# A convolution's weight-gradient loads moved ahead of the last input-gradient stage, with twelve row buffers in place of four

## The chip, the cores and the metric

One core of a Trainium2 chip. The metric is the device time of one execution in microseconds (us); each figure is the median of several executions. The kernel before takes 2702.24 us (5 runs, 2699.1 to 2705.55).

## The reference

A strided 1-D convolution, a normalisation over time, GELU, and the gradients of all of it. B = 2 batches, T = 16000 samples, 256 channels, K = 31 taps, stride 2, L = 7985 outputs.

```python
for i in range(K):                               # forward
    h += einsum('blc,cd->bld', x[:, i:i+s*L:s, :], w[i])
h = (h - mu) / sqrt(var + 1e-5) * gn_gamma + gn_beta
return gelu(h)
# and its vector-Jacobian product with grad_out: gradients of x, w, gamma, beta
```

## The kernel before

It runs in three phases, all bound to TensorE. Forward convolution of batch 0, then of batch 1 (the elementwise work of batch 0 runs beside it); input-gradient convolution of batch 0 (the elementwise work of batch 1 beside it), then of batch 1; weight gradient in four segments. TensorE is called PE in the views, ScalarE ACT, VectorE DVE, GpSimd POOL and SyncE SP. The tiles named most: `pt`, the PSUM banks into which TensorE transposes; `row`, `xrow` and `wrow`, rows in SBUF on their way out (results and intermediates, input gradient, weight gradient); `osl` and `gT`, what is transposed for out_0 and gh_dram; `w_sb` and `wT_sb`, the weights of phase 1 and 2; `xg` and `gseg`, the two operands of one weight-gradient segment; `sg`, a sigmoid. The pools:

```python
# phase 1 and 2: pools, on two sides of SBUF; "stg" holds rows on their way out
big   = tc.tile_pool(name="big",   bufs=3)                     # left side
wpool = tc.tile_pool(name="wpool", bufs=1,  side="right")      # w_sb, later wT_sb
xtp   = tc.tile_pool(name="xtp",   bufs=16, side="right")
temps = tc.tile_pool(name="temps", bufs=2,  side="right")
otp   = tc.tile_pool(name="otp",   bufs=4,  side="right")
stg   = tc.tile_pool(name="stg",   bufs=4,  side="right")      # tags "row" and "xrow"
ps_tr = tc.tile_pool(name="ps_tr", bufs=2, space=PSUM)         # pt
...
def transpose_and_store(srcs, b, l0, N, dram_dst):             # out_0 and gh_dram
    for q in range(_cdiv(N, P)):
        pt = ps_tr.tile([P, NDD, P], BF16, name="pt")
        for dd in range(NDD):
            nc.tensor.transpose(out=pt[0:M, dd, :], in_=srcs[dd][...], identity=ident[:])  # L262
        row = stg.tile([P, D], BF16, name="row")
        nc.scalar.copy(out=row[0:M, :], in_=pt[...])                                       # L264
        nc.gpsimd.dma_start(out=dram_dst[...], in_=row[0:M, :])                            # L265
...
def conv_backward_x(b):                                        # input gradient, L480
    ...  # 30 or 32 matmuls into acc_x; scalar.copy to xrow (L489); gpsimd store (L490)
...
# the elementwise work of the last batch: a slab's transposes follow its arithmetic by "lag" steps
items_last = new_sched(elementwise_items(last), lag=8)
# phase 3, after those pools are closed
seg = tc.tile_pool(name="seg", bufs=2, side="right")
for b in range(B):
    for h in range(NH):
        xg   = seg.tile([P, RW, C], BF16, name="xg")           # 46.5 KB a partition
        gseg = seg.tile([P, SH, D], BF16, name="gseg")         # 16 KB a partition
        ...  # six loads of gseg from gh_dram (L574), six of xg from x (L582), on the SP queue
        for grp in groups:                                     # 8 taps, one PSUM bank each
            ...  # matmuls acc_w (L600); VectorE adds into gw_acc, the last segment into wrow
```

A scheduler orders each engine's instructions from this program and places the waits by the addresses that tiles share. A pool that is opened later over the addresses of a closed one waits for the last use of what lay there.

## Time and profile before

| what (kernel before) | us | where to read it |
|---|---|---|
| span | 2701.7 | page |
| PE busy | 2611.7 (97%) | page |
| PE waits for xg, once | 25.3 | waits of PE |
| PE waits for rows leaving pt, 26 times | 25.9 | waits of PE |
| ScalarE waits for row stores | 27.5 + 7.6 | waits of ACT |

A busy TensorE cannot be made shorter by this change, since no matmul is removed. What can be won is its idle time, and the slow clock after idle time. So the first view to read is the waits of PE in the kernel before: who waited for whom, us in total, times, longest.

```profile
PE pt L262 <- ACT row L264: 25.9, 26, 3.9
PE acc_w L600 <- DMA xg<-in_x_dram: 25.3, 1, 25.3
PE acc_f L212 <- DMA w_sb<-in_w_dram: 9.7, 1, 9.7
PE acc_w L600 <- DVE wrow L618: 6.5, 3, 2.5
PE acc_x L480 <- DMA wT_sb<-in_w_dram: 3.1, 3, 2.5
```

The same view for ScalarE (ACT) says what most of the first line is: the copy out of pt has no free row to write to until an earlier row has reached memory.

```profile
ACT row L264 <- DMA gh_dram<-row: 27.5, 33, 2.5
...
ACT row L264 <- DMA out_dram<-row: 7.6, 5, 2.1
```

The second line of PE is one event. The chain of waits of the kernel before (start, length, what) shows it step by step: the last output store lands, only then does the SP queue issue the loads, 22 us later the data is there.

```profile
1784.41 1.78 DMA out_dram<-xrow
1786.19 0.02 SPq L574
...
1786.88 21.98 DMA xg<-in_x_dram
...
1808.99 51.09 PE acc_w L600 x452
```

The windows view of the kernel before (window, its length, then busy time and count of PE, PEld, DVE, ACT, POOL, then the granted clock, DMA share, GB/s) shows that the stall goes on costing after it ended: the clock has dropped to 0.50, and the first matmuls run at half pace (10 in 2 us, later 21).

```profile
1805.00:1809.00 4.00, 0.01 (x1) 0.04 (x2) 0.00 (x0) 0.00 (x0) 0.00 (x0) 0.50 0.29 122
1809.00:1811.00 2.00, 2.00 (x10) 1.45 (x11) 0.00 (x0) 0.00 (x0) 0.00 (x0) 0.50 0.33 126
1811.00:1813.00 2.00, 2.00 (x15) 1.54 (x14) 0.00 (x0) 0.00 (x0) 0.00 (x0) 0.68 0.32 129
1813.00:1815.00 2.00, 2.00 (x21) 1.80 (x19) 0.00 (x0) 0.00 (x0) 0.00 (x0) 1.00 0.32 126
```

The same view with windows cut at five events gives the stages. The events are the first gh_dram transpose, the last transposes of out_0, the last transposes of gh_dram, the end of the input gradient, and the first weight-gradient matmul.

```profile
0.00:865.30 865.30, 846.16 (x4018) 394.16 (x4096) 263.65 (x763) 136.30 (x379) 36.50 (x79) 1.00 0.29 58
865.30:1234.40 369.10, 347.09 (x3172) 303.67 (x3171) 263.43 (x757) 114.41 (x293) 118.48 (x218) 0.98 0.20 50
1234.40:1317.50 83.10, 78.66 (x757) 68.70 (x757) 0.00 (x0) 28.11 (x85) 44.78 (x85) 1.00 0.22 67
1317.50:1784.00 466.50, 466.17 (x4264) 417.99 (x4263) 0.00 (x0) 51.82 (x140) 75.88 (x141) 1.00 0.07 21
1784.00:1809.00 25.00, 0.01 (x1) 0.04 (x2) 0.00 (x0) 0.12 (x1) 6.82 (x2) 0.59 0.28 111
1809.00:2701.70 892.70, 873.65 (x7936) 778.56 (x7936) 81.37 (x155) 0.00 (x0) 39.42 (x63) 0.99 0.11 38
```

In the second stage lies one more stall worth a look, from the order of instructions in time (start, length, engine, line, what, and in brackets the idle time before it and its releaser): PE waits 3.86 us for a row copy, and ScalarE, which owes it, had itself been idle for 5.91 us, waiting for VectorE.

```profile
972.42 0.63 ACT L286 ACTIVATE sg<-inner 128x512 bf16<-128x512 bf16 x1 [5.91 <-DVE inner L283]
...
973.20 0.65 ACT L264 COPY row<-pt 128x256 bf16<-128x256 bf16 x2
...
973.63 0.37 PE L262 MATMUL pt<-ident,osl 128*128 128x128 bf16 x2 [3.86 <-ACT row L264]
```

### The profile page before, as it was taken

How to read it: one execution, taken by the hardware profiler on the slowest of the kernel's cores; microseconds unless marked ns; L12 is line 12 of the kernel's file. 1: busy time of each engine (PE TensorE's matmuls, PEld its weight loads, DVE VectorE, ACT ScalarE, POOL GpSimd, SP SyncE). 2: the span in 40 equal slices, each digit the busy share in tenths (PEclk: the TensorE clock that was granted, in tenths of full speed). 3: DMA queues.
4: the chain of work that ended last, by engine and by line, in shares of the span. 5: the costliest groups of instructions: out<-in, count | busy, mean ns of one | idle time of the engine just before them, and what ended most of it. 6: DMA issues, size and time to landing. Idle time of an engine off the chain costs nothing.

```text
span 2701.7 us, 45421 instructions
## 1 busy us (share of the span) xinstructions
PE 2611.7 (97%) x20143; PEld 1963.1 (73%) x20220; DVE 608.4 (23%) x1675; ACT 330.8 (12%) x895; POOL 321.9 (12%) x586
## 2 busy tenths in 40 slices
PE   8999999999999899999999999969999999999997
PEld 3444445444445688888888888858888888888886
DVE  0000005755571886770000000000001000100001
ACT  0010102222211522222211111100000000000000
POOL 0000000000001522234411111110000000000112
PEclk9999999999999999999999999989999999999999
DMA  5212123432225401111100000022102002100000
GB/s 113 45 38 43 39 40 69 80 59 45 55 55 104 102 30 34 32 34 51 52 20 20 19 20 22 22 77 102 68 1 120 1 1 64 57 1 1 17 17 30
DMA packets 221422, 121.51 MB, mean 45 GB/s; under 512 B 198218, under 2 KB 206188, under 8 KB 220724
## 3 DMA queue, kind: packets, MB, share of 16 engines
q1 hardware_dynamic: 202984, 81.74, 12.8%
q0 software_dynamic: 18240, 36.85, 4.6%
q8 instruction: 158, 2.59, 0.4%
q14 instruction: 40, 0.33, 0.0%
HBM read 36.04 MB, written 36.82 MB: 27 GB/s over the span
## 4 chain that ended last, share of the span: by engine, by line
PE 69%; issue 20%; POOL 4%; DVE 2%; DMA 2%; ACT 1%; SPq 0%; POOLq 0%; ACTq 0%; DVEq 0%
PE acc_w L600 26%; PE acc_x L480 24%; PE acc_f L212 18%; POOL gh_dram L265 1%; POOL out_dram L620 1%; DMA gh_dram<-row 1%; POOL out_dram L490 1%; DMA xg<-in_x_dram 1%; POOL out_dram L265 1%; ACT row L264 1%; PE pt L262 0%; DMA out_dram<-row 0%; DVE gT L355 0%; DVE junk_v L362 0%; DVE inner L283 0%
## 5 line engine op out<-in xcount | busy, mean ns | idle before, releaser
L600 PE MATMUL acc_w<-gseg,xg 125*128 125x256 bf16 x7936 | 873.7, 273 | 32.0 <-DMA xg<-in_x_dram 25.3
L480 PE MATMUL acc_x<-wT_sb,gT 128*128 128x256 bf16 (+1 forms) x7812 | 882.0, 274 | 3.1 <-DMA wT_sb<-in_w_dram 3.1
L600 PEld LDWEIGHTS <-xg 125*128 125x128 bf16 x7936 | 778.6, 98 | 127.0 <-issue 33.3
L212 PE MATMUL acc_f<-xt,w_sb 128*128 128x512 bf16 (+1 forms) x3891 | 840.5, 374 | 13.8 <-DMA w_sb<-in_w_dram 9.7
L480 PEld LDWEIGHTS <-gT 128*128 128x128 bf16 (+1 forms) x7812 | 762.3, 98 | 90.7 <-issue 5.0
L212 PEld LDWEIGHTS <-w_sb 128*128 128x128 bf16 x3968 | 385.0, 97 | 453.4 <-DMA w_sb<-in_w_dram 9.7
L490 POOL DMA_DIRECT2D out_dram<-xrow x252 | 137.0, 544 | 634.7 <-ACT xrow L489 564.9
L612 DVE COPY gw_acc<-acc_w 128x512 f32<-128x512 f32 x31 | 18.9, 682 | 805.9 <-PE acc_w L600 805.9
L489 ACT CAST xrow<-acc_x 128x256 bf16<-128x256 f32 (+1 forms) x252 | 93.3, 371 | 614.9 <-PE acc_x L480 603.3
L265 POOL DMA_DIRECT2D out_dram<-row x126 | 68.0, 545 | 811.8 <-ACT row L264 801.4
L614 DVE TENSOR_TENSOR gw_acc<-acc_w,gw_acc 128x512 f32<-128x512 f32 x62 | 37.8, 683 | 396.3 <-PE acc_w L600 396.3
L237 DVE TENSOR_REDUCE hsum<-hsum_part 128x2 f32<-128x32 f32 x2 | 0.4, 186 | 477.6 <-ACT hT L221 477.6
L221 ACT ACTIVATE hT<-acc_f 128x512 bf16<-128x512 f32 (+1 forms) x64 | 37.5, 586 | 550.4 <-PE acc_f L212 550.4
L264 ACT COPY row<-pt 128x256 bf16<-128x256 bf16 (+1 forms) x252 | 86.6, 379 | 45.4 <-DMA gh_dram<-row 27.5
L620 POOL DMA_DIRECT2D out_dram<-wrow x62 | 33.1, 539 | 413.5 <-DVE wrow L618 412.6
L265 POOL DMA_DIRECT2D gh_dram<-row x126 | 67.7, 543 | 42.7 <-ACT row L264 35.0
L618 DVE TENSOR_TENSOR wrow<-acc_w,gw_acc 128x256 bf16<-128x256 f32 x62 | 24.6, 422 | 207.5 <-PE acc_w L600 186.1
L561 POOL MEMSET xg<- 32x7424 bf16 x2 | 12.6, 6279 | 453.8 <-PE acc_w L600 452.0
L288 DVE TENSOR_TENSOR osl<-z,sg 128x512 bf16<-128x512 bf16 (+1 forms) x64 | 25.1, 416 | 175.8 <-PE pt L262 164.8
L286 ACT ACTIVATE sg<-inner 128x512 bf16<-128x512 bf16 (+1 forms) x64 | 39.7, 621 | 166.8 <-DVE inner L283 158.2
L262 PE MATMUL pt<-ident,gT 128*128 128x128 bf16 (+1 forms) x252 | 32.5, 222 | 17.9 <-ACT row L264 16.6
L340 ACT ACTIVATE sg<-inner 128x512 bf16<-128x512 bf16 (+1 forms) x64 | 39.7, 621 | 74.5 <-DVE inner L337 72.5
(73 smaller groups left out, 761.7 us busy)
## 6 DMA issues: line engine op xcount, KB each, us to landing
out_dram<-xrow POOLq DMA_DIRECT2D x248, 64.0 KB, 1.8
out_dram<-row POOLq DMA_DIRECT2D x124, 64.0 KB, 2.6
gh_dram<-row POOLq DMA_DIRECT2D x124, 64.0 KB, 1.8
gseg<-gh_dram SPq DMA_DIRECT2D x16, 375.0 KB
xg<-in_x_dram SPq DMA_DIRECT2D x8, 750.0 KB
xg<-in_x_dram SPq DMA_DIRECT2D x8, 744.0 KB
xg<-in_x_dram SPq DMA_DIRECT2D x2, 2312.5 KB
xg<-in_x_dram SPq DMA_DIRECT2D x2, 2294.0 KB
```

The costliest lines, as they stand in the source:

```text
L212: nc.tensor.matmul(accs[dd][:, 0:N], lhsT=w_sb[:, cc, i, dd * P:(dd + 1) * P], rhs=rhs, start=(n == 0), stop=(n == total - 1),)
L221: nc.scalar.activation(out=hT_b[:, dd, PADL + l0:PADL + l0 + N], in_=accs[dd][:, 0:N], func=ACT.Copy, accum_out=hsum_part[b][:, dd, lt:lt ...
L264: nc.scalar.copy(out=row[0:M, :], in_=pt[0:M].rearrange("p k d -> p (k d)"))
L265: dma_out.dma_start(out=dram_dst[b, l0 + c0:l0 + c0 + M, :], in_=row[0:M, :])
L286: nc.scalar.activation(out=sg[:, 0:N], in_=inner[:, 0:N], func=ACT.Sigmoid, scale=GELU_K)
L340: nc.scalar.activation(out=sg[:, 0:N], in_=inner[:, 0:N], func=ACT.Sigmoid, scale=GELU_K)
L480: nc.tensor.matmul(acc[0:Mu, 0:C], lhsT=gT_b[:, dd, PADL + u0 - m:PADL + u0 - m + Mu], rhs=wT_sb[:, dd, i, :], start=(n == 0), stop=(n == ...
L489: nc.scalar.copy(out=xrow[0:Mu, :], in_=acc[0:Mu, 0:C])
L490: dma_out.dma_start(out=out_1[b, bass.ds(2 * u0 + par, Mu, step=2), :], in_=xrow[0:Mu, :])
L600: nc.tensor.matmul(accs[ti][:, cc, :], lhsT=xg[0:NG, 2 * s + i, cc * P:(cc + 1) * P], rhs=gseg[0:NG, s, :], start=(cnt[ti] == 0), stop=(cn ...
L614: nc.vector.tensor_tensor(out=dst, in0=src_ps, in1=dst, op=ALU.add)
L620: dma_out.dma_start(out=out_2[i, cc * P:(cc + 1) * P, :], in_=wrow[:])
```

## The change

Its intent: load the first weight-gradient segment while the last input gradient still runs, into the space of the elementwise pools, which are no longer needed by then; and give the rows on their way out more buffers. To make the room, the weights and the rows move to the left side, and the two segment buffers become two pools. The loading code moves into a function, unchanged, and stg3, the pool of wrow, moves to the left too (both cut).

```diff
-        wpool = ph12.enter_context(tc.tile_pool(name="wpool", bufs=1, side="right"))
-        xtp = ph12.enter_context(tc.tile_pool(name="xtp", bufs=16, side="right"))
-        temps = ...; otp = ...                                  # side="right"
-        stg = ph12.enter_context(tc.tile_pool(name="stg", bufs=4, side="right"))
+        wpool = ph12.enter_context(tc.tile_pool(name="wpool", bufs=1))
+        stg = ph12.enter_context(tc.tile_pool(name="stg", bufs=12))
+        phE = ExitStack()                    # xtp, temps, otp: closed early
+        xtp = phE.enter_context(tc.tile_pool(name="xtp", bufs=16, side="right"))
+        temps = ...; otp = ...
 ...
             else:                            # last batch
+                phE.close()
+                segA = tc.alloc_tile_pool(name="segA", bufs=1, side="right")
+                segA_holder[0] = segA
+                seg_first[0] = bw_load_segment(segA, *bw_segments[0])
                 for _ in conv_backward_x(b):
                     pass
 ...
-        seg = ph3.enter_context(tc.tile_pool(name="seg", bufs=2, side="right"))
+        segB = tc.alloc_tile_pool(name="segB", bufs=1, side="right")
+        seg_pools = [segA, segB]             # segments take turns; the first one is already loaded
```

More of the change, by code (lines that the diff above doesn't have):

```diff
@@ L119, with bw_load_segment @@
             r0 += rn
+    GRP = 8
+    groups = [list(range(i0, min(K, i0 + GRP))) for i0 in range(0, K, GRP)]
+    def bw_load_segment(pool, b, h):
+        xg = pool.tile([P, RW, C], BF16, name="xg", tag="xg")
+        gseg = pool.tile([P, SH, D], BF16, name="gseg", tag="gseg")
+        g_last = NG - 1
+        max_r_last = T - 1 - (2 * SB * g_last + 2 * SH * h)
+        nfull = NG if max_r_last >= RW - 1 else NG - 1
+        if nfull < NG:
+            qb0 = (g_last // 32) * 32
+            r_inv0 = max(0, max_r_last + 1)
+            nc.gpsimd.memset(xg[qb0:qb0 + 32, r_inv0:RW, :], 0.0)
+        s_bounds = sorted(set([0] + [min(SH, v) for v in (4, 8, 14, 20, 26)] + [SH]))
+        r_prev = 0
+        for pi in range(len(s_bounds) - 1):
+            s_lo, s_hi = s_bounds[pi], s_bounds[pi + 1]
+            if s_hi <= s_lo:
+                continue
+            r_hi = min(RW, 2 * (s_hi - 1) + K)
+            gsrc = bass.AP(
+                tensor=gh_dram.tensor,
+                offset=gh_dram[b, SH * h + s_lo, 0].offset,
+                ap=[[SB * D, NG], [1, (s_hi - s_lo) * D]],
+            )
+            dma_in.dma_start(out=gseg[0:NG, s_lo:s_hi, :].rearrange("g s d -> g (s d)"), in_=gsrc)
+            if r_hi > r_prev:
+                if nfull > 0:
+                    src = bass.AP(
+                        tensor=x.tensor,
+                        offset=x[b, 2 * SH * h + r_prev, 0].offset,
+                        ap=[[2 * SB * C, nfull], [1, (r_hi - r_prev) * C]],
+                    )
+                    dma_in.dma_start(out=xg[0:nfull, r_prev:r_hi, :].rearrange("g r c -> g (r c)"), in_=src)
+                if nfull < NG:
+                    nv = min(max_r_last + 1, r_hi)
+                    if nv > r_prev:
+                        t0 = 2 * SB * g_last + 2 * SH * h
+                        dma_in.dma_start(
+                            out=xg[g_last:g_last + 1, r_prev:nv, :],
+                            in_=x[b, t0 + r_prev:t0 + nv, :].rearrange("(o r) c -> o r c", o=1),
+                        )
+                r_prev = r_hi
+        return xg, gseg
@@ L121 @@
+    bw_segments = [(b, h) for b in range(B) for h in range(NH)]
+    seg_first = [None]
+    segA_holder = [None]
     with ExitStack() as ph12:
         big = ph12.enter_context(tc.tile_pool(name="big", bufs=3))
-        wpool = ph12.enter_context(tc.tile_pool(name="wpool", bufs=1, side="right"))
-        xtp = ph12.enter_context(tc.tile_pool(name="xtp", bufs=16, side="right"))
-        temps = ph12.enter_context(tc.tile_pool(name="temps", bufs=2, side="right"))
-        otp = ph12.enter_context(tc.tile_pool(name="otp", bufs=4, side="right"))
@@ L131 @@
+        temps = phE.enter_context(tc.tile_pool(name="temps", bufs=2, side="right"))
+        otp = phE.enter_context(tc.tile_pool(name="otp", bufs=4, side="right"))
         w_sb = wpool.tile([P, NCC, K, D], BF16, name="w_sb", tag="w")
@@ L530 @@
             else:
+                phE.close()
+                segA = tc.alloc_tile_pool(name="segA", bufs=1, side="right")
+                segA_holder[0] = segA
+                seg_first[0] = bw_load_segment(segA, *bw_segments[0])
                 for _ in conv_backward_x(b):
                     pass
+        phE.close()
     ggam_bf = const.tile([P, NDD], BF16, name="ggam_bf")
@@ L543 @@
         accp = ph3.enter_context(tc.tile_pool(name="accp", bufs=1))
-        seg = ph3.enter_context(tc.tile_pool(name="seg", bufs=2, side="right"))
-        stg3 = ph3.enter_context(tc.tile_pool(name="stg3", bufs=4, side="right"))
+        stg3 = ph3.enter_context(tc.tile_pool(name="stg3", bufs=4))
+        if segA_holder[0] is None:
+            segA_holder[0] = tc.alloc_tile_pool(name="segA", bufs=1, side="right")
+        segA = segA_holder[0]
+        segB = tc.alloc_tile_pool(name="segB", bufs=1, side="right")
@@ L546 @@
         ps_w = ph3.enter_context(tc.tile_pool(name="ps_w", bufs=8, space=bass.MemoryType.PSUM))
-        GRP = 8
-        groups = [list(range(i0, min(K, i0 + GRP))) for i0 in range(0, K, GRP)]
         gw_acc = accp.tile([P, K, NCC * D], FP32, name="gw_acc")
-        first_seg = True
-        for b in range(B):
-            for h in range(NH):
-                xg = seg.tile([P, RW, C], BF16, name="xg", tag="xg")
-                gseg = seg.tile([P, SH, D], BF16, name="gseg", tag="gseg")
-                g_last = NG - 1
-                max_r_last = T - 1 - (2 * SB * g_last + 2 * SH * h)
-                nfull = NG if max_r_last >= RW - 1 else NG - 1
-                if nfull < NG:
-                    qb0 = (g_last // 32) * 32
-                    r_inv0 = max(0, max_r_last + 1)
-                    nc.gpsimd.memset(xg[qb0:qb0 + 32, r_inv0:RW, :], 0.0)
-                s_bounds = sorted(set([0] + [min(SH, v) for v in (4, 8, 14, 20, 26)] + [SH]))
-                r_prev = 0
-                for pi in range(len(s_bounds) - 1):
-                    s_lo, s_hi = s_bounds[pi], s_bounds[pi + 1]
-                    if s_hi <= s_lo:
-                        continue
-                    r_hi = min(RW, 2 * (s_hi - 1) + K)
-                    gsrc = bass.AP(
-                        tensor=gh_dram.tensor,
-                        offset=gh_dram[b, SH * h + s_lo, 0].offset,
-                        ap=[[SB * D, NG], [1, (s_hi - s_lo) * D]],
-                    )
-                    dma_in.dma_start(out=gseg[0:NG, s_lo:s_hi, :].rearrange("g s d -> g (s d)"), in_=gsrc)
-                    if r_hi > r_prev:
-                        if nfull > 0:
-                            src = bass.AP(
-                                tensor=x.tensor,
-                                offset=x[b, 2 * SH * h + r_prev, 0].offset,
-                                ap=[[2 * SB * C, nfull], [1, (r_hi - r_prev) * C]],
-                            )
-                            dma_in.dma_start(out=xg[0:nfull, r_prev:r_hi, :].rearrange("g r c -> g (r c)"), in_=src)
-                        if nfull < NG:
-                            nv = min(max_r_last + 1, r_hi)
-                            if nv > r_prev:
-                                t0 = 2 * SB * g_last + 2 * SH * h
-                                dma_in.dma_start(
-                                    out=xg[g_last:g_last + 1, r_prev:nv, :],
-                                    in_=x[b, t0 + r_prev:t0 + nv, :].rearrange("(o r) c -> o r c", o=1),
-                                )
-                        r_prev = r_hi
-                last_seg = (b == B - 1) and (h == NH - 1)
-                for grp in groups:
-                    accs = [ps_w.tile([P, NCC, D], FP32, name="acc_w", tag="accw") for _ in grp]
-                    total_per_bank = SH * NCC
-                    cnt = [0] * len(grp)
-                    for s in range(SH):
-                        for ti, i in enumerate(grp):
-                            for cc in range(NCC):
-                                nc.tensor.matmul(
-                                    accs[ti][:, cc, :],
-                                    lhsT=xg[0:NG, 2 * s + i, cc * P:(cc + 1) * P],
-                                    rhs=gseg[0:NG, s, :],
-                                    start=(cnt[ti] == 0),
-                                    stop=(cnt[ti] == total_per_bank - 1),
-                                )
-                                cnt[ti] += 1
-                    for ti, i in enumerate(grp):
-                        dst = gw_acc[:, i, :]
-                        src_ps = accs[ti][:].rearrange("p k d -> p (k d)")
-                        if first_seg:
-                            nc.vector.tensor_copy(out=dst, in_=src_ps)
-                        elif not last_seg:
-                            nc.vector.tensor_tensor(out=dst, in0=src_ps, in1=dst, op=ALU.add)
-                        else:
-                            for cc in range(NCC):
-                                wrow = stg3.tile([P, D], BF16, name="wrow", tag="wrow")
@@ new lines @@
+        seg_pools = [segA, segB]
+        nseg = len(bw_segments)
+        for si, (b, h) in enumerate(bw_segments):
+            if si == 0 and seg_first[0] is not None:
+                xg, gseg = seg_first[0]
+            else:
+                xg, gseg = bw_load_segment(seg_pools[si % 2], b, h)
+            first_seg = si == 0
+            last_seg = si == nseg - 1
+            for grp in groups:
+                accs = [ps_w.tile([P, NCC, D], FP32, name="acc_w", tag="accw") for _ in grp]
+                total_per_bank = SH * NCC
+                cnt = [0] * len(grp)
+                for sidx in range(SH):
+                    for ti, i in enumerate(grp):
+                        for cc in range(NCC):
+                            nc.tensor.matmul(
+                                accs[ti][:, cc, :],
+                                lhsT=xg[0:NG, 2 * sidx + i, cc * P:(cc + 1) * P],
+                                rhs=gseg[0:NG, sidx, :],
+                                start=(cnt[ti] == 0),
+                                stop=(cnt[ti] == total_per_bank - 1),
+                            )
+                            cnt[ti] += 1
+                for ti, i in enumerate(grp):
+                    dst = gw_acc[:, i, :]
+                    src_ps = accs[ti][:].rearrange("p k d -> p (k d)")
+                    if last_seg:
+                        for cc in range(NCC):
+                            wrow = stg3.tile([P, D], BF16, name="wrow", tag="wrow")
+                            if first_seg:
+                                nc.vector.tensor_copy(out=wrow[:], in_=accs[ti][:, cc, :])
+                            else:
@@ L618 @@
                                 nc.vector.tensor_tensor(out=wrow[:], in0=accs[ti][:, cc, :],
                                                         in1=gw_acc[:, i, cc * D:(cc + 1) * D], op=ALU.add)
-                                dma_out.dma_start(out=out_2[i, cc * P:(cc + 1) * P, :], in_=wrow[:])
-                first_seg = False
-        if B * NH == 1:
-            for i in range(K):
-                for cc in range(NCC):
-                    wrow = stg3.tile([P, D], BF16, name="wrow", tag="wrow")
-                    nc.vector.tensor_copy(out=wrow[:], in_=gw_acc[:, i, cc * D:(cc + 1) * D])
-                    dma_out.dma_start(out=out_2[i, cc * P:(cc + 1) * P, :], in_=wrow[:])
+                            dma_out.dma_start(out=out_2[i, cc * P:(cc + 1) * P, :], in_=wrow[:])
+                    elif first_seg:
+                        nc.vector.tensor_copy(out=dst, in_=src_ps)
+                    else:
+                        nc.vector.tensor_tensor(out=dst, in0=src_ps, in1=dst, op=ALU.add)
@@ L631 @@
+        segB.release()
+        segA.release()
 _INS = ['x', 'w', 'gn_gamma', 'gn_beta', 'grad_out']
```

## The prediction

> **What bounds it now.** TensorE: PE is 97% busy of 2701.7 us on the page. In undisturbed stretches of the windows view 2013 weight-gradient matmuls take 220 us (0.109 us each). The change removes no matmul, so it can gain only PE idle time and slow clock. The waits of PE sum to about 70 us: 25.3 us once, for the load of xg; 25.9 us in 26 pieces, transposes into pt waiting for ScalarE's copy to row; 9.7 us for w_sb; 6.5 us for wrow; 3.1 us for wT_sb.
>
> **Step 1: the first segment's loads go ahead of the last input-gradient convolution.** Before, they wait for the last store of xrow: the chain of waits ends it at 1786.19, then shows 21.98 us of DMA, and PE starts at 1808.99. In the built order the new loads wait for the first 128 stores of the software queue (batch 0) and for elementwise work that ended near 1235 us, so they have 550 us to land. What remains is the last copy of an accumulator (ScalarE, 1783.76 for 0.37 us): about 0.5 us idle. Gain 24.8 us.
> The idle PE also loses clock: 0.50 granted from 1790 to about 1812, where the first 25 matmuls take 4 us in place of 2.7. The Trainium skill ("TensorE: Matmul & The Clock Gate", Part 1) says that an idle array falls to half rate and needs about 3.4 us of activity to return; this trace agrees. Gain 1.5 us. Together 26 us.
>
> **Step 2: row buffers go from 4 to 12.** ScalarE's copies wait 27.5 us for gh_dram stores and 7.6 us for out stores; most of PE's 25.9 us is this, passed on. Not all comes back:
> - 500 to 800 us: 5.2 us of pt waits, about 3 back, since two pt banks leave PE pacing on a 0.37 us copy.
> - 1250 to 1310 us: 3.4 us, about 3 back. POOL needs 0.54 us for each of 15 stores per 10 us, and fits.
> - 865 to 975 us: about 17 us. The new order packs the 63 gh_dram groups against about 150 input-gradient matmuls, before about 280. Stores pace it at 0.54 us, overlapping the wT_sb load to 886 us. PE leaves the burst about 10 us earlier, but then meets VectorE, busy 92 us between 870 and 980: the 3.86 us wait ending at 973.6 is ScalarE waiting for a sigmoid input, ahead of the copies in its queue. Buffers don't speed VectorE. I expect 5 us back, 0 to 12.
> Together 11 us.
>
> **Nothing else moves.** Segment 1 is loaded after the convolution, as before, with 220 us of matmuls to hide behind. The waits for wrow, w_sb and wT_sb stay. Instruction counts are equal.
>
> **Sum.** 26 + 11 = 37 us: 2702 becomes 2664 us, range 2650 to 2678. Faster by over 2% (under about 2649) 9%, within 2% 90%, slower 1%.
>
> **What would show each step.** Step 1: PE's wait for xg under 2 us, clock 1.0 across the stage change, gseg and xg issued near 1240 us. Step 2: ScalarE's waits for row stores fall from 35 to under 8 us; PE's pt waits fall from 25.9 to about 12, the largest near 960 to 975 us and traced to VectorE; POOL issues about 18 stores per 10 us around 890.
>
> **What would make it wrong.** The packed burst could stall PE longer than before, with half-clock stretches after each stall: then only 26 us in all. Or VectorE gains, because ScalarE no longer blocks its sigmoids: then 12 us there, about 2655.

## The result, and the profile after

The changed kernel takes 2661.34 us (median of 7, 2659.07 to 2664.1); the kernel before, run beside it, 2700.8 us (13 runs). The ratio is 0.9853, with a 95% interval of 0.9843 to 0.9863. A ratio here is the mean of one kernel's fast runs over that of the other's of the same rounds, so it is not quite the ratio of the medians. The gain of 1.5% is clear of the noise.

The waits of PE in the changed kernel (its line numbers are 50 or so higher for the same statements):

```profile
PE pt L312 <- ACT row L314: 11.8, 7, 3.3
PE acc_f L262 <- DMA w_sb<-in_w_dram: 9.6, 1, 9.6
PE acc_x L530 <- DMA wT_sb<-in_w_dram: 6.7, 6, 2.2
PE acc_w L622 <- DVE wrow L639: 6.2, 3, 2.5
PE acc_w L622 <- ACT xrow L539: 0.5, 1, 0.5
```

The wait for xg is gone; what is left in its place is 0.5 us for the last accumulator's copy. ScalarE no longer waits for any row store that is worth a line: the row copy's own wait is now for PE.

```profile
ACT row L314 <- PE pt L312: 7.9, 13, 2.0
```

The chain of waits of the changed kernel at the same place runs straight through:

```profile
1764.94 7.55 PE acc_x L530 x68
1772.50 0.03 ACTq L539
...
1772.56 0.37 ACT xrow L539
...
1772.98 7.04 PE acc_w L622 x63
```

And the stages by the windows view of the changed kernel, cut at the same events:

```profile
0.00:865.70 865.70, 848.24 (x4017) 394.92 (x4095) 263.27 (x763) 136.76 (x379) 36.64 (x79) 1.00 0.29 58
865.70:1226.50 360.80, 344.27 (x3173) 303.01 (x3171) 262.32 (x757) 113.45 (x293) 118.23 (x218) 0.98 0.19 52
1226.50:1306.30 79.80, 78.48 (x757) 68.67 (x757) 0.00 (x0) 27.53 (x85) 44.85 (x85) 1.00 0.45 170
1306.30:1772.50 466.20, 466.18 (x4264) 418.05 (x4264) 0.00 (x0) 51.57 (x139) 75.92 (x141) 1.00 0.07 21
1772.50:1773.00 0.50, 0.02 (x1) 0.03 (x2) 0.00 (x0) 0.37 (x1) 0.00 (x0) 1.00 0.00 0
1773.00:2662.30 889.30, 870.74 (x7936) 777.02 (x7935) 81.37 (x155) 0.00 (x0) 46.19 (x65) 0.99 0.09 33
```

Subtracting the lengths gives the account of the 39.4 us between the two profiled spans: forward stage -0.4, second stage 8.3, batch-1 stores 3.3, rest of the input gradient and the stage change 24.8 together (0.3 and 24.5), weight gradient 3.4. Note the third line: that stage now carries 170 GB/s in place of 67, because the early load falls into it, and still got shorter.

The -0.4 of the forward stage hides a gain. PE's row waits in this stage fell from 5.2 to 3.6 us. But after one of them, in this one profile, the granted clock was 0.59 and then 0.56 (684 to 686 and 686 to 688 us by the windows view), and 110 matmuls of the forward convolution took 26.21 us in place of 24.60. First the kernel before, then the changed kernel:

```profile
684.42 24.60 PE L212 MATMUL acc_f<-xt,w_sb 128*128 128x512 bf16 x110
...
684.07 0.65 PE L312 MATMUL pt<-ident,osl 128*128 128x128 bf16 x4 [1.85 <-ACT row L314]
684.51 26.21 PE L262 MATMUL acc_f<-xt,w_sb 128*128 128x512 bf16 x110
```

No other profile has a slow stretch there; most have the same wait, of 1.83 or 1.84 us. So I take the loss of 1.6 us for an accident of this profile and not for an effect of the change.

The stall on VectorE is still there, 6.6 us earlier and at 3.28 in place of 3.86 us; ScalarE's idle time before it is the same 5.91 us. In order of time, changed kernel:

```profile
965.80 0.63 ACT L336 ACTIVATE sg<-inner 128x512 bf16<-128x512 bf16 x1 [5.91 <-DVE inner L333]
...
966.59 1.44 ACT L314 COPY row<-pt 128x256 bf16<-128x256 bf16 x4
...
967.02 0.27 PE L312 MATMUL pt<-ident,osl 128*128 128x128 bf16 x2 [3.28 <-ACT row L314]
```

A second one of the same kind, of 2.73 us, is new at 942 us.

### The profile page after: what moved, and what is told of

The parts are those of the page before. It is cut to its first block, busy times and chain, and to the rows that moved or that the text cites. A ratio compares the mean times of both kernels' runs of the same rounds, so it can differ in the third digit from the quotient of the medians.

```text
span 2662.3 us, 45400 instructions
## 1 busy us (share of the span) xinstructions
PE 2607.9 (98%) x20143; PEld 1961.7 (74%) x20220; DVE 607.0 (23%) x1675; ACT 329.7 (12%) x895; POOL 321.8 (12%) x586
## 4 chain that ended last, share of the span: by engine, by line
PE 87%; issue 6%; DVE 3%; POOL 1%; DMA 1%; ACT 1%; SPq 1%; ACTq 0%; POOLq 0%; DVEq 0%
PE acc_x L530 31%; PE acc_f L262 29%; PE acc_w L622 26%; POOL out_dram L641 1%; PE pt L312 1%; SPq L562 1%; ACT row L314 0%; DMA gh_dram<-row 0%; DMA wT_sb<-in_w_dram 0%; DVE junk_v L412 0%; DVE inner L387 0%; DVE gT L405 0%; DVE inner L333 0%; DMA out_dram<-wrow 0%; SPq L210 0%
## 5 line engine op out<-in xcount | busy, mean ns | idle before, releaser
L622 PEld LDWEIGHTS <-xg 125*128 125x128 bf16 x7936 | 777.1, 98 | 100.4 <-issue 8.3
L448 DVE SCALAR_TENSOR_TENSOR gT<-y,bbcoef,tq 128x512 bf16<-128x512 bf16 (+1 forms) x64 | 46.5, 729 | 0.0
```

What stands on the lines that cost most here:

```text
L448: nc.vector.scalar_tensor_tensor(out=gseg, in0=y[:, 0:N], scalar=bbcoef[b][:, dd:dd + 1], in1=tq[:, 0:N], op0=ALU.mult, op1=ALU.add)
L622: nc.tensor.matmul(accs[ti][:, cc, :], lhsT=xg[0:NG, 2 * sidx + i, cc * P:(cc + 1) * P], rhs=gseg[0:NG, sidx, :], start=(cnt[ti] == 0), st ...
```

## The experiments

Twelve kernels ran, all with correct results, each with five rounds against the kernel before on the same chip (4 or 5 executions gave a time). The table collects what the profiles showed, in stage lengths: F up to the first gh_dram transpose, S2 up to the last out_0 transposes, S3 (the batch-1 gh_dram stores) up to the last gh_dram transposes, S4 up to the first weight-gradient matmul, W to the end. Each is the difference of two times in that kernel's profile. F is 864.4 to 866.0 us in the four profiles with four rows and 862.1 to 863.9 us in those with eight or twelve, but for the changed kernel's own 865.7 with its slow stretch. So the rows, with the order made for them, are worth about 2 us there; smaller differences are not read as effects.

| kernel | median us | ratio to before (95%) | F | S2 | S3 | S4 | W |
|---|---|---|---|---|---|---|---|
| before | 2700 to 2704 | 1 | 865.3 | 369.1 | 83.1 | 491.5 | 892.7 |
| changed | 2661.34 | 0.9853 (0.9843-0.9863) | 865.7 | 360.8 | 79.8 | 466.7 | 889.3 |
| e1_early_only | 2687.06 | 0.9952 (0.9940-0.9965) | 864.4 | 366.7 | 97.9 | 466.6 | 888.7 |
| e2_rows_only | 2687.68 | 0.9955 (0.9941-0.9969) | 863.4 | 360.0 | 79.8 | 491.6 | 891.0 |
| e3b_layout_pools | 2689.60 | 0.9957 (0.9945-0.9970) | 865.7 | 368.5 | 100.4 | 466.6 | 889.5 |
| e9_late_code | 2659.73 | 0.9849 (0.9835-0.9862) | 863.4 | 361.7 | 79.8 | 466.6 | 887.0 |
| e11_early_held | 2672.08 | 0.9897 (0.9882-0.9912) | 866.0 | 365.7 | 82.3 | 466.7 | 888.3 |
| e12_after_held | 2662.72 | 0.9868 (0.9852-0.9885) | 862.4 | 362.6 | 79.8 | 466.7 | 888.1 |
| e13_rows8 | 2663.08 | 0.9858 (0.9843-0.9873) | 863.9 | 360.0 | 80.4 | 466.7 | 888.2 |
| e5_pt3 | 2659.21 | 0.9850 (0.9835-0.9864) | 862.1 | 357.5 | 79.6 | 467.1 | 889.7 |
| e6_lag14 | 2658.36 | 0.9846 (0.9832-0.9861) | | | | | |
| e7_wrow16 | 2650.81 | 0.9813 (0.9798-0.9828) | 862.9 | 358.6 | 79.8 | 466.7 | 878.9 |
| e14_best | 2654.45 | 0.9821 (0.9803-0.9838) | | | | | |
| e15_lag14_wrow16 | 2650.10 | 0.9806 (0.9792-0.9819) | | | | | |

(With a longer lag the out_0 transposes end later, so S2 and S3 are cut at other work and are left out.)

### The two halves apart

e1_early_only: the changed kernel with the old number of rows.

```diff
-        stg = ph12.enter_context(tc.tile_pool(name="stg", bufs=12))
+        stg = ph12.enter_context(tc.tile_pool(name="stg", bufs=4))
```

> The changed kernel with 4 row buffers, so the early load alone. If the two parts add up, the stage change gives 24.8 us of idle plus 1.7 us of half clock, and perhaps up to 2 us in the tail: 2672 to 2675 us against about 2701; PE's waits for row copies stay near 26 us, its wait for xg is gone. If the parts depended on each other (the early load only useful behind the freed rows), it would be nearer 2685.

e2_rows_only: the kernel before with twelve rows.

```diff
-        stg = ph12.enter_context(tc.tile_pool(name="stg", bufs=4, side="right"))
+        stg = ph12.enter_context(tc.tile_pool(name="stg", bufs=12, side="right"))
```

> The kernel before with 12 row buffers, so the buffers alone. The end of the last convolution came 11.2 us earlier in the changed kernel (1783.7 to 1772.5): if that is the buffers alone, 2688 to 2691 us, with the xg wait still 25 us and ScalarE's waits for row stores under 4 us. If instead the moved pools or the early load caused the 11 us, it stays at 2699 to 2703.

The buffers alone did what they should: 2687.68 us, the wait for xg still 25.4 us, S2 and S3 as in the changed kernel. (With twelve rows the scheduler also orders PE's transposes and matmuls differently up to about 930 us, so in F and S2 the gain is that of the buffers with the order made for them; no run separates the two. In S3 the order is the same.) The early load alone missed its range by 12 us. S4 shows its full 24.9 us, but S3 became 14.8 us longer than before. Against about 2700, the halves gain 13.0 and 12.4 us (25.4 in all), together 39.5: some 14 us appear only when both are there. PE's waits for row copies rose from 25.9 to 36.0 us, and ScalarE's for gh_dram stores from 27.5 to 41.0 us, although PE goes through the same sequence of transposes and matmuls in the traces of e1_early_only and of the kernel before. The waits of e1_early_only:

```profile
PE pt L312 <- ACT row L314: 36.0, 29, 3.9
...
ACT row L314 <- DMA gh_dram<-row: 41.0, 48, 3.6
```

### Does the place in the program matter, or the place in memory?

Does the load have to be written early to be issued early? Two kernels test it. e3b_layout_pools is the kernel before with only the pools moved, the loading code left in phase 3:

```diff
-        wpool = ...(name="wpool", bufs=1, side="right"))
+        wpool = ...(name="wpool", bufs=1))
-        stg = ...(name="stg", bufs=4, side="right"))
+        stg = ...(name="stg", bufs=4))
-        seg = ...(name="seg", bufs=2, side="right"))
+        segA = ...(name="segA", bufs=1, side="right"))
+        segB = ...(name="segB", bufs=1, side="right"))
+                seg = segA if (b * NH + h) % 2 == 0 else segB
```

> The kernel before with the weights and row pools on the other side and the two segment buffers in two pools; the load stays where it stood in the program, after the convolution. Theory space: only the address of the segment buffer, laid over rows and weights still in use, held the load back, so it goes out near 1240 to 1320 us all the same and the time is 2672 to 2675. Theory program order: the load must be written ahead of the convolution, so it stays at 2699 to 2703 with a 25 us wait for xg.

e9_late_code is the changed kernel without the early call:

```diff
-                segA = tc.alloc_tile_pool(name="segA", bufs=1, side="right")
-                segA_holder[0] = segA
-                seg_first[0] = bw_load_segment(segA, *bw_segments[0])
```

> The changed kernel without the early call; the first segment is allocated and loaded in the third phase. Theory space: 2660 to 2663 as the changed kernel, load issued near 1230 us. Theory program order: the 26 us come back, 2686 to 2690.

Space won on both. In e3b_layout_pools the wait for xg is gone and the first gseg load goes out at 1234.5 us. Its waits of PE and the issues of gseg (duration min/median/max in ns, first and last start):

```profile
PE pt L262 <- ACT row L264: 38.9, 34, 3.9
...
PE acc_w L602 <- ACT xrow L489: 0.5, 1, 0.5
...
L576 SPq DMA_DIRECT2D gseg<-gh_dram x24: 257/2998/10102, 1234.5 to 2289.8; - x24
```

Its time, 2689.6, missed the expected 2672 for the reason that e1_early_only missed it: four rows, and S3 at 100.4 us. e9_late_code is as fast as the changed kernel. So the effective part of "issue it early" is that segA lies over xtp, temps and otp, and no longer over weights and rows that are in use until 1786 us. (Moving the pools and splitting the segment buffers in two were not tried one by one.)

### Where did the early load alone lose its 14 us?

My theory after these runs: the load, which goes out near 1230 us, meets the batch-1 gh_dram stores. The time from issue to landing in the stretch 1247 to 1315 us supports it (issue, count, KB each, median us to landing). The kernel before:

```profile
gh_dram<-row POOLq DMA_DIRECT2D x58, 64.0 KB, 1.8
```

e1_early_only:

```profile
gh_dram<-row POOLq DMA_DIRECT2D x48, 64.0 KB, 5.0
```

The changed kernel:

```profile
gh_dram<-row POOLq DMA_DIRECT2D x58, 64.0 KB, 5.0
```

The stores are equally slow in the last two; in this stage PE's order is the same, and only the number of rows that can wait for them differs. To test it, e11_early_held holds the load back until those stores are done, by first touching each piece with a one-row copy that reads the last gh_dram row of batch 1 (the load then overwrites it):

```diff
+            if (b, h) == (0, 0):
+                late = gh_dram[B - 1, L - 1:L, :]
+                dma_in.dma_start(out=gseg[0:1, s_lo, :], in_=late)
+                if r_hi > r_prev:
+                    dma_in.dma_start(out=xg[0:1, r_prev, :], in_=late)
             dma_in.dma_start(out=gseg[0:NG, s_lo:s_hi, :]..., in_=gsrc)
```

> Four row buffers and the early load, as in e1_early_only, but each piece of the first segment is first touched by a one-row copy that reads the last gh_dram row of batch 1, so that the load goes out only after the batch-1 stores, near 1320 us. Theory collision: in e1_early_only the load made those stores slower, which four row buffers passed on to PE (row waits 36 us, the stage of the batch-1 stores 98 us in place of 83); held back, the row waits fall to about 26 us and the time to 2672 to 2675. Theory layout: the moved pools themselves cost e1 its 13 us; then it stays at 2685 to 2689.

It came to 2672.08 us, S3 to 82.3 us, PE's row waits to 24.8 us, ScalarE's for gh_dram stores to 27.3 us. Landing in the same stretch is back:

```profile
gh_dram<-row POOLq DMA_DIRECT2D x61, 64.0 KB, 1.8
```

The moved pools are the same as in e1_early_only and e3b_layout_pools, so the rival (the layout itself) falls. e12_after_held puts the same hold into the changed kernel:

> The changed kernel with the same hold. Theory collision: twelve buffers already hide the slower stores (79.8 us for that stage with and without the load), so holding gains nothing: 2658 to 2662. If collisions still cost the changed kernel PE time, it comes to 2655 or less.

It gained nothing (2662.72, just over its range), S3 is 79.8 us with and without the load: twelve rows hide the collision fully. e13_rows8 asks how many are needed:

```diff
-        stg = ph12.enter_context(tc.tile_pool(name="stg", bufs=12))
+        stg = ph12.enter_context(tc.tile_pool(name="stg", bufs=8))
```

> The changed kernel with 8 row buffers. If the loss of e1_early_only is a matter of how many stores can be under way while the load runs, 8 buffers hide most of it: row waits of PE 12 to 17 us, stage of the batch-1 stores 80 to 84 us, 2661 to 2667. If anything under 12 fails, nearer 2680.

Eight nearly do: 2663.08 us and S3 80.4 us. The Trainium skill ("DMA: Bandwidth & Descriptors", Issuing engines are not separate DMA queues) says that transfers started by different engines end up on the same 16 DMA engines and interleave there. This trace agrees: the load is on the SP queue, the stores on the POOL queue, and the stores' landing goes from 1.8 to 5.0 us. The same page's rules advise to issue a DMA early and wait for it late; e1_early_only is a case where following this cost 15 us against e11_early_held (the ratios 0.9952 and 0.9897 say the same), because short transfers that PE depended on were under way then.

### What keeps the rest of the row waits?

Two reasons stood in the prediction. The first, two pt banks, was tested by e5_pt3:

```diff
-        ps_tr = ...(name="ps_tr", bufs=2, space=PSUM)
+        ps_tr = ...(name="ps_tr", bufs=3, space=PSUM)
```

> The changed kernel with three pt banks in PSUM in place of two. The prediction held that two banks pace PE in the 500 to 800 us stage, where the waits of 1.8 us at 544 and 684 us stayed: with three they fall under 1 us each, 2657 to 2659. If those waits come from ScalarE being busy with other work, they stay and the time is 2659 to 2662.

The time, 2659.21, lies 0.2 us above the range for "two banks pace PE" and inside the one for "ScalarE is busy with other work", and the waits that a third bank should have removed stayed. In order of time, PE in e5_pt3:

```profile
542.92 0.27 PE L312 MATMUL pt<-ident,osl 128*128 128x128 bf16 x2 [1.44 <-ACT row L314]
682.53 0.27 PE L312 MATMUL pt<-ident,osl 128*128 128x128 bf16 x2 [1.59 <-ACT row L314]
```

They were 1.77 and 1.85 us with two banks. The trace of the changed kernel suggests why: ScalarE sits idle for 6.83 us until 540.67, waiting for a sigmoid input, and then takes four accumulator copies and squares before the row copies that PE waits for (543.49). It is the order in ScalarE's queue behind a VectorE wait; no run here changes that order in the forward stage, so this reading is not tested.

The second reason, VectorE, was tested by e6_lag14:

```diff
-        items_last = new_sched(elementwise_items(last), lag=8)
+        items_last = new_sched(elementwise_items(last), lag=14)
```

> The changed kernel with the transposes of the batch-1 elementwise slabs issued 14 steps after their arithmetic in place of 8. Theory VectorE: the waits of 2.7 and 3.3 us at 942 and 967 us are ScalarE's queue held by sigmoids that wait for VectorE, which is over 99% busy from 910 to 970; six steps (20 us) more of slack remove both and a half-clock stretch: 2652 to 2656. Theory PSUM or row buffers: lag does not matter, waits stay near 6 us, 2659 to 2662.

Both waits (2.73 and 3.28 us) are gone and the pt waits fell from 11.8 to 5.7 us, so slack against VectorE is what they needed. The time fell less than expected: 2658.36 lies between the ranges of the two theories. It is about 4 us under e12_after_held, but the intervals of the two ratios overlap. Part of it came back as a new PE idle of 1.85 us at 1222, after which the clock was 0.67 and 0.50 up to 1226 us.

### Beyond both kernels

e7_wrow16 gives the same remedy to the other store buffers, the rows of the weight gradient:

```diff
-        stg3 = ph3.enter_context(tc.tile_pool(name="stg3", bufs=4))
+        stg3 = ph3.enter_context(tc.tile_pool(name="stg3", bufs=16))
```

> The changed kernel with 16 buffers for wrow in place of 4, the same remedy at the end of the program. VectorE's waits for wrow stores (18 us) go, a bank of eight is emptied in about 5.7 us in place of 8.5, PE's three waits shrink from 6.2 us to about 3, and the drain after the last matmul shortens by about 1.3 us: 2655 to 2658, against 2660 to 2663 if PE's waits are only the order of banks.

It did better: 2650.81 us. I had sized PE's wait by VectorE's pace over a bank and kept 3 us of it; in fact all three waits (6.2 us) vanished. W fell by 10.4 us. Of these 6.2 are the waits and 1.4 the shorter drain (from the last matmul's start to the end 11.1 us in place of 12.5). The remaining 2.8 are PE's busy time on the same matmuls (870.7 and 867.9 us). A half-clock stretch after the last wait of the changed kernel makes 1.6 of it: the last 428 matmuls took 48.73 us there, and 47.09 in e9_late_code, where no slow clock followed the same wait of 2.54 us. About 1.2 us stay open.

e14_best and e15_lag14_wrow16 add the longer lag to this, the first with three pt banks as well:

> The changed kernel with lag 14, three pt banks and 16 wrow buffers together. Added up from the single runs (about 3, 2 and 4 us): 2650 to 2655. If they share one wait, 2656 to 2658.

> The changed kernel with lag 14 and 16 wrow buffers, two pt banks as before. If the three pt banks were what kept e14_best from adding up (its waits of 4.0 and 3.4 us are in neither single run), this adds 4 us of lag to the 2651 of e7_wrow16: 2646 to 2649, over 2% faster than the kernel before. If lag is worth nothing once measured again: 2650 to 2653.

Neither came out better than e7_wrow16 within the intervals: e14_best came to 2654.45 and e15_lag14_wrow16 to 2650.10 us. The first lies in the range for adding up, but this had counted the 16 buffers at 4 us, and they gave more alone; the second lies in the range for "lag is worth nothing". In e15_lag14_wrow16 PE idles once more near the end of the batch-1 elementwise work:

```profile
1226.05 14.12 PE L530 MATMUL acc_x<-wT_sb,gT 128*128 128x256 bf16 x101 [3.53 <-issue]
...
1229.40 1.11 POOL L315 DMA_DIRECT2D out_dram<-row  x2 [9.96 <-DMA out_dram<-ggam_bf]
```

The POOL queue stands for 10 us behind the small store of the gamma gradient. The kernel with lag 8 has that wait too (9.3 us), but nobody on PE needs the queue at that moment; with lag 14 the last out_0 rows do. This is read from the trace and was not tested by a run. The best versions, at ratios of 0.981 with intervals that reach over 0.98, are not clearly beyond the 2% mark.

## Why the prediction was right or wrong

It named 2664 us (2650 to 2678); the measured time is 2661.3. Term by term, from the stage lengths:

| term of the sum | predicted us | measured us | held up by |
|---|---|---|---|
| wait for xg replaced by 0.5 us | 24.8 | 24.8 (S4) | e1, e3b, e9, e11: S4 466.6 to 466.7 |
| half clock after that wait | 1.5 | about 1.3 | clock 1.00 at the stage change; 25 matmuls in 4 us cost that much at 0.109 us each |
| rows, 500 to 800 us | 3 | 1.6 less waiting (5.2 to 3.6); F -0.4 with the slow stretch | e2: waits 3.6, F 1.9 shorter |
| rows, 865 to 1235 us | 5 (0 to 12) | 8.3 (S2) | e2: 9.1 |
| rows, batch-1 stores | 3 | 3.3 (S3) | e2: 3.3 |
| nothing else moves | 0 | about 2 (W); wT_sb waits 3.6 longer, inside S2 | a slow stretch of the kernel before; not tested |

Step 1 was right in size. It named the wait (the last store of xrow) and left open why the load had it; e9_late_code and e3b_layout_pools show that the address does it and not the place in the program. The prediction's signs came in: loads issued at 1226.8 us (said: near 1240), PE's pt waits 11.8 us (said: about 12), ScalarE's row-store waits gone, 19 POOL instructions between 890 and 900 us (said: about 18), and the largest remaining pt wait at 967 us.

The term that was mis-sized, and whose reason failed, is "500 to 800 us: 5.2 us of pt waits, about 3 back, since two pt banks leave PE pacing". 1.6 us came back. The waits there were 1.77 and 1.85 us afterwards, and a third bank left 1.44 and 1.59, so pacing by two banks accounts for 0.6 of the 3.6 us. A smaller miss: "the waits for wrow, w_sb and wT_sb stay" does not hold for wT_sb, for which PE waited 6.7 us in place of 3.1, all of it in S2. The rows as a whole came to 11.2 us (-0.4, 8.3, 3.3) against 11 said; that this fits so well is luck, since F fell short by 3.4 us (1.6 of it the slow stretch) and S2 came out 3.3 us over the estimate.

One thing was missed although the total did not show it. I treated the two steps as a sum, and gave the early load no cost. Taken alone it costs some 15 us in S3 (e1_early_only against e11_early_held), which exactly the other half of the change pays for. The sum was right only because both halves were made together; a prediction of the first half by itself, from the same reasoning, was wrong by 12 us. In S2 the buffers did better than my estimate, inside its range. The picture held: PE's pt waits in S2 fell from 17.2 to 8.2 us because the burst of gh_dram transposes stalled less (up to 930 us 2.2 in place of 13.2 us), and PE then met VectorE, where one wait of 3.86 us became two of 2.73 and 3.28. With 3.6 us more for wT_sb and 2.8 us less busy time for the same matmuls (the clock was 0.95 in place of 0.93 from 865 to 990 us) this makes 8.2 of the 8.3 us. VectorE's waits for sigmoids (the osl and oms lines of its waits) fell too, from 18.7 to 10.9 us, as in the upside that the prediction had named; but PE's waits on VectorE did not shrink, so that this upside paid is not shown.

The last 2 us of W lie between the wrow waits at the end. In the kernel before the clock was 0.57 from 2580 to 2584 us, after a wait of 2.15 us, and the 512 matmuls that follow took 57.66 us; in the changed kernel they took 56.24 after a wait of 2.02. That is 1.4 us, and the waits themselves are 0.3 us shorter. Nothing in the change touches this place, so I take it for chance in single profiles; it was not tested.

## What to carry to other kernels

When a load is late, look at which addresses it waits for before moving the line of code: what lies under its buffer decides when it can start. When a load is moved earlier, ask which short transfers it will now meet, and whether their buffers are enough for the longer landing: here 1.8 us became 5.0, four buffers lost 15 us and eight lost almost nothing. Test the parts of a change alone as well as together, since the sum of parts and the whole differed here by a third of the gain.

## What the Trainium skill lacked or had wrong

- "DMA: Bandwidth & Descriptors", Rules for kernel authors: the rule to issue a DMA early has no warning about transfers that are under way then. Here an early load made 64 KB stores land in 5.0 us in place of 1.8 and cost 15 us with four row buffers (2687.1 against 2672.1 us), nothing with twelve.
- No page that I found gives a way to size store buffers from the landing time. Here 4, 8 and 12 rows gave 97.9, 80.4 and 79.8 us for the same stage beside the load.
- "TensorE: Matmul & The Clock Gate", Part 1, puts the return of the full clock at about 3.4 us of activity, and this agrees (1809.0 to about 1812.3 us, worked out from the 0.68 between 1811 and 1813). It puts the drop at an idle window of about 3.4 us, and tells, without a length, of a kernel whose frequent short idles did it too; here an idle of 1.85 us was followed by a clock of 0.59 and then 0.56 (684 to 688 us, changed kernel) and one of 3.28 us by 0.66 and then 0.50, but one of 2.73 us by 1.00 (942 to 946 us). So one idle shorter than the window can be enough, and its length alone does not tell.
